# Sketched attention and a Swish-beta MLP on one core: the kernel rewritten with products on halves of the TensorE array, a key sum from ones columns, a first piece of 256 tokens, chunks of 512 tokens and a written order

## The chip, the cores and the metric

The kernel runs on one core of one Trainium2 chip. TensorE (PE) multiplies matrices into PSUM, its weight loads are profiled apart (PEld); VectorE (DVE) and ScalarE (ACT) read PSUM and SBUF, GpSimd (POOL) works on SBUF, SyncE (SP) issues most of the DMAs. The metric is the device time of one execution in microseconds. The kernel before took 153.2 us as the median of 3 runs (152.99 to 153.49).

## The reference

q, k and v are (4 batches, 4 heads, 1088 tokens, 32) float32, S1 and S2 are (8, 32). A sketch phi turns each 32-vector into 64 features, the attention is linear in them, and its output goes token by token into an MLP of width 2048.

```python
def phi(x):
    a = einsum('rd,bhsd->bhsr', S1, x)
    b = einsum('rd,bhsd->bhsr', S2, x)
    return einsum('bhsi,bhsj->bhsij', a, b).reshape(..., 64)
q_p, k_p = phi(q), phi(k)
kv  = einsum('bhsf,bhsd->bhfd', k_p, v)
z   = sum(k_p, axis=2)
num = einsum('bhsf,bhfd->bhsd', q_p, kv)
den = einsum('bhsf,bhf->bhs', q_p, z)[..., None] + 1e-06
x   = (num / den).transpose(0, 2, 1, 3).reshape(4352, 128)
h   = x @ w_in                                # (4352, 2048)
out = (h / (1 + exp(-beta * h))) @ w_out      # (4352, 128) float32
```

## The kernel before

The attention is computed in float32, the MLP in float16. A float32 matmul shows as two records in the profile, one for each of its two passes over the columns, and so do its weight loads; a float16 matmul shows as one.

Per batch, `attention(b)` makes a list of steps. Keys are transposed on VectorE in 32x32 blocks (`kT`, line 191), projected with S1 and S2 (`kproj`: `tk` or `tka`, line 216, nine matmuls, 128 weight columns, 64 moving columns), copied to SBUF (`tkS`) and multiplied to features `kp` (line 254, on POOL except in batch 0). `zt` (line 280, nine matmuls) and `wps` (line 298) make the key sum z in the form of eight more projection columns for the queries. `kvp` (line 314) adds up kv: 18 matmuls, of which those of heads 0 and 1 write PSUM partitions 0 to 63 and those of heads 2 and 3 partitions 64 to 127, so each uses 64 of the 128 columns of the array. Then three chunks of 384, 352 and 352 tokens of each head follow: `abp` (line 355) projects the queries, line 364 transposes that, lines 370 to 378 compute the denominator and divide, line 391 makes the query features `qp`, line 402 transposes them, and `xps` (line 411) multiplies them with kv in two accumulating matmuls. The result is cast to float16 as `xT`. In batch 0 the same tiles are called `abw` and `xw`, and ScalarE makes the copies.

`moe(b, ci)` takes one such chunk of 384 or 352 tokens through the MLP in eight waves: two matmuls into a `wave` of two PSUM banks (line 463), one Silu over both banks (line 466), and, two waves later, the two matmuls of the second product into `acc` (line 443). `winp` is w_in times beta and `woutp` is w_out divided by beta, so that Silu is all that is left. After the eighth wave `osb` (line 448) transposes `acc` and four DMAs write it out.

The order: attention of batch 0 is written whole ahead of the MLP; afterwards the steps of batch b+1 are spread evenly over the 24 waves of batch b, and a scheduler places the instructions of the engines by priority and readiness. The pools have two buffers of `wave`, of `att` and of `acc` in PSUM.

Of the kernel before, what the change touches and what calls it, by code (L numbers as in the profile page):

```python
# [10 lines left out]
ACTF = mybir.ActivationFunctionType  # L11

P = 128
# [4 lines left out]
def kernel(  # L18
# [12 lines left out]

# [4 lines left out]
    F = R * R  # L38
# [4 lines left out]
    assert DM == H * D == P and D == T and S == U * T and R == 8  # L43

    C = U // 4
    UL = U - 4 * C
    NB = C + 1
    assert UL == 2
    u_chk = []
    o = 0  # L50
    for n in (12, 11, 11):
        u_chk.append((o, n))
        o += n
    assert o == U
    NMAX = 12 * T

    const = ctx.enter_context(tc.tile_pool(name="const", bufs=1))
    sb = ctx.enter_context(tc.tile_pool(name="sb", bufs=2))
    ps = ctx.enter_context(tc.tile_pool(name="ps", bufs=2, space=bass.MemoryType.PSUM))

    def ap3(t, offset, dims):
        return bass.AP(tensor=t.tensor, offset=t.offset + offset, ap=[list(t.ap[0])] + dims)


    q_in = [const.tile([P, U * D], F32, tag=f"q_in{b}", name=f"q_in{b}") for b in range(B)]
    k_in = [const.tile([P, U * D], F32, tag=f"k_in{b}", name=f"k_in{b}") for b in range(B)]
    v_in = [const.tile([P, H, NB, D], F32, tag=f"v_in{b}", name=f"v_in{b}") for b in range(B)]
# [3 lines left out]
    def load_v(b, eng):  # L71
        for uu in range(4):
            eng.dma_start(
                out=v_in[b][T * uu : T * uu + T, :, 0:C, :].rearrange("p h c d -> p h (c d)"),
                in_=bass.AP(
                    tensor=v.tensor,
                    offset=v.offset + b * H * S * D + uu * C * D,
                    ap=[[U * D, T], [S * D, H], [1, C * D]],
                ),
            )  # L80
        for uu in range(UL):
            eng.dma_start(
                out=v_in[b][T * uu : T * uu + T, :, C, :],
                in_=bass.AP(
                    tensor=v.tensor,
                    offset=v.offset + b * H * S * D + (4 * C + uu) * D,
                    ap=[[U * D, T], [S * D, H], [1, D]],
                ),
            )

    nc.sync.dma_start(out=k_in[0], in_=k_rows[0])


    s_in = const.tile([P, P], F32, tag="s_in")
    nc.vector.memset(s_in, 0.0)
    s2bd = const.tile([2 * H * R, P], F32, tag="s2bd")
    nc.vector.memset(s2bd, 0.0)
    for h in range(H):
        nc.scalar.dma_start(out=s_in[T * h : T * h + R, T * h : T * h + T], in_=S1)
        nc.scalar.dma_start(out=s_in[T * h + R : T * h + 2 * R, T * h : T * h + T], in_=S2)  # L100
    load_v(0, nc.sync)
    nc.sync.dma_start(out=q_in[0], in_=q_rows[0])
    for h in range(H):
        nc.scalar.dma_start(out=s2bd[2 * R * h + R : 2 * R * h + 2 * R, T * h : T * h + T], in_=S2)


    bmask = const.tile([P, P], F32, tag="bmask")
    nc.gpsimd.memset(bmask, 0.0)
    for h in range(H):
        nc.gpsimd.memset(bmask[T * h : T * h + T, T * h : T * h + T], 1.0)  # L110
    zmask = const.tile([2 * H * R, H, R], F32, tag="zmask")
    nc.gpsimd.memset(zmask, 1.0)
    nc.gpsimd.affine_select(
        out=zmask, in_=zmask, pattern=[[-2 * R, H], [0, R]], base=0, channel_multiplier=1,
        compare_op=ALU.is_ge, fill=0.0,
    )
    nc.gpsimd.affine_select(
        out=zmask, in_=zmask, pattern=[[2 * R, H], [0, R]], base=2 * R - 1, channel_multiplier=-1,
        compare_op=ALU.is_ge, fill=0.0,
    )  # L120


    wq = []
    for i in range(2):
        w = const.tile([P, H, T], F32, tag=f"wq{i}", name=f"wq{i}")
        nc.vector.transpose(out=w.rearrange("p h r -> p (h r)"), in_=s_in)  # L126
        wq.append(w)
    prod = []
    for i in range(2):
        m = const.tile([P, 12, R + 1], F32, tag=f"prod{i}", name=f"prod{i}")  # L130
        nc.vector.memset(m[:, :, R : R + 1], 1e-6)
        prod.append(m)


    winp = const.tile([P, DFF], F16, tag="winp")
    woutp = const.tile([P, NJ, P], F16, tag="woutp")
    beta_bc = const.tile([P, DFF], F32, tag="beta_bc")
    w_in_sb = const.tile([P, DFF], F32, tag="w_in_sb")
    w_out_sb = const.tile([P, NJ, P], F32, tag="w_out_sb")
    betat = const.tile([P, NJ], F32, tag="betat")  # L140
    rbetat = const.tile([P, NJ], F32, tag="rbetat")
    nc.sync.dma_start(out=w_in_sb, in_=moe_w_in)
    nc.sync.dma_start(
        out=beta_bc,
        in_=bass.AP(tensor=moe_beta.tensor, offset=moe_beta.offset, ap=[[0, P], [1, DFF]]),
    )
    with nc.allow_non_contiguous_dma(reason="strided beta gather (one time)"):
        nc.scalar.dma_start(out=betat, in_=moe_beta.rearrange("(j p) -> p j", p=P))
    nc.sync.dma_start(out=w_out_sb, in_=moe_w_out.rearrange("(j p) m -> p j m", p=P))
    for b in range(1, B):  # L150
        nc.sync.dma_start(out=k_in[b], in_=k_rows[b])
        load_v(b, nc.sync)
        nc.sync.dma_start(out=q_in[b], in_=q_rows[b])
    HF = DFF // 2
    for i in range(2):
        nc.gpsimd.tensor_tensor(
            out=winp[:, i * HF : i * HF + HF],
            in0=w_in_sb[:, i * HF : i * HF + HF],
            in1=beta_bc[:, i * HF : i * HF + HF],
            op=ALU.mult,  # L160
        )

    def scale_w_out():
        nc.vector.reciprocal(out=rbetat, in_=betat)
        for j in range(NJ):
            nc.scalar.activation(
                out=woutp[:, j, :], in_=w_out_sb[:, j, :], func=ACTF.Copy, scale=rbetat[:, j : j + 1]
            )

    xts = {}  # L170


    def attention(b):
        first = b == 0
        st = {}
        steps = []

        def step(f):
            steps.append(f)

        def evac(o, i):
            if first:
                nc.scalar.copy(out=o, in_=i)  # L183
            else:
                nc.vector.tensor_copy(out=o, in_=i)  # L185

        @step
        def _():
            st["kT"] = sb.tile([P, U, T], F32, tag="kT", name="kT")
            kT = st["kT"]  # L190
            nc.vector.transpose(
                out=ap3(kT, 0, [[1, C * P]]), in_=ap3(k_in[b], 0, [[D, C], [C * D, 4], [1, D]])
            )
            nc.vector.transpose(
                out=ap3(kT, C * P, [[1, UL * T]]), in_=ap3(k_in[b], 4 * C * D, [[1, UL * D]])
# [36 lines left out]
        for c0 in range(0, NB, 3):  # L232
            @step
            def _(c0=c0):
                for c in range(c0, min(NB, c0 + 3)):
                    kproj(c)
# [280 lines left out]
```

## Time and profile before

| | |
|---|---|
| median of 3 runs | 153.2 us (152.99 to 153.49) |
| span of the profiled execution, first to last instruction | 151.3 us |
| outside of it, against the median | 1.9 us |
| PE busy | 125.2 us, 83% of the span |
| ScalarE busy / VectorE busy / POOL busy | 76.8 / 72.7 / 27.5 us |
| mean granted TensorE clock | 0.94 of full |
| first Silu ends | 50.7 us |
| last matmul ends | 146.8 us |

The profile gives no time of the profiled execution apart from its span, so the 1.9 us are the median less the span. Matmul rows overlap, since they are pipelined: what a group of matmuls costs is read from the chain of work that ended last, where a group's entry runs from its start to the next group's start. "x16" on a line is a count of records, two for each float32 matmul. The page's slices are 3.8 us each.

### The profile page before, as it was taken

To read this page: it belongs to the slowest core of one execution; us is meant where nothing else is said; L and a number is where in the kernel's file an instruction comes from. 1 tells how busy PE (TensorE), PEld (TensorE's weight loads), DVE (VectorE), ACT (ScalarE), POOL (GpSimd) and SP (SyncE) were. 2 spreads that over 40 slices of the span, in tenths; PEclk is the share of its full clock that TensorE was granted. 3 is DMA by queue.
4 is the path that set the end of the run, shared out by engine and by line. 5 is a ranking of instruction groups with operands and counts; after the bars stand their busy time and mean duration, and the time that the engine had idled before them with its cause. 6 is when DMAs were issued, how large, how long until landed. Compare 5 with 4: busy or idle time off the path is not lost.

```text
span 151.3 us, 2035 instructions
## 1 busy us (share of the span) xinstructions
PE 125.2 (83%) x752; PEld 78.3 (52%) x752; DVE 72.7 (48%) x163; ACT 76.8 (51%) x120; POOL 27.5 (18%) x33
## 2 busy tenths in 40 slices
PE   0058880959977599999999999999999999999970
PEld 0057750438553355655586565555865555555530
DVE  0313739085099904195922165965322857831110
ACT  0031039100102969884915487746335848669960
POOL 3023890005941000000009200000380000000000
PEclk9999996595599779999999999999999999999998
DMA  4649999996000000220200302020002020203122
GB/s 147 109 146 410 364 317 319 285 334 178 0 2 0 0 0 17 42 48 0 47 1 4 52 0 45 3 40 12 0 13 43 0 50 0 48 0 52 19 36 48
DMA packets 25866, 12.22 MB, mean 81 GB/s; under 512 B 22016, under 2 KB 24064, under 8 KB 25600
## 3 DMA queue, kind: packets, MB, share of 16 engines
q1 hardware_dynamic: 23600, 12.06, 29.4%
q10 hardware_dynamic: 2256, 0.02, 0.9%
q8 instruction: 6, 0.10, 0.3%
q14 instruction: 4, 0.03, 0.1%
HBM read 9.85 MB, written 2.23 MB: 80 GB/s over the span
## 4 chain that ended last, share of the span: by engine, by line
PE 60%; DVE 20%; ACT 9%; DMA 4%; issue 2%; ACTq 0%; DVEq 0%
PE wave L463 14%; PE acc L443 12%; PE xps L411 8%; ACT gT L466 8%; PE kvp L314 6%; PE xw L411 5%; DVE qp L391 4%; PE tka L216 4%; DMA betat<-in_moe_beta_dram 3%; DVE qpt L402 3%; PE abp L355 3%; PE zt L280 3%; DVE ab L364 3%; PE tk L216 2%; DVE kp L254 2%
## 5 line engine op out<-in xcount | busy, mean ns | idle before, releaser
L466 ACT ACTIVATE gT<-wave 128x704 f16<-128x704 f32 (+1 forms) x96 | 67.2, 775 | 29.2 <-PE wave L463 29.2
L463 PE MATMUL wave<-xT,winp 128*128 128x352 f16 (+1 forms) x192 | 46.9, 322 | 1.9 <-ACT gT L466 1.6
L443 PE MATMUL acc<-gT,woutp 128*128 128x352 f16 (+1 forms) x192 | 46.1, 322 | 0.2 <-ACT gT L466 0.2
L254 POOL TENSOR_TENSOR kp<-tkS 128x1024 f32<-128x1024 f32 (+2 forms) x11 | 15.7, 1453 | 75.0 <-DVE tkS L185 71.3
L463 PEld LDWEIGHTS <-winp 128*128 128x128 f16 x192 | 18.4, 99 | 19.6 <-issue 8.3
L443 PEld LDWEIGHTS <-woutp 128*128 128x128 f16 x192 | 18.7, 98 | 12.0 <-issue 1.8
L448 DVE STREAM_TRANSPOSE osb<-acc 128x352 f32<-128x352 f32 (+1 forms) x12 | 6.7, 558 | 16.6 <-PE acc L443 16.6
L411 PE MATMUL xps<-qpt,kv 128*128 128x352 f32 (+1 forms) x36 | 13.4, 489 | 0.4 <-DVE qpt L402 0.3
L185 DVE CAST xT<-xps 128x352 f16<-128x352 f32 (+1 forms) x9 | 4.8, 535 | 15.2 <-PE xps L411 15.2
L183 ACT CAST xT<-xw 128x352 f16<-128x352 f32 (+1 forms) x3 | 1.4, 461 | 21.0 <-PE xw L411 21.0
L391 DVE TENSOR_TENSOR qp<-an,ab 128x352 f32<-128x352 f32 (+1 forms) x24 | 11.8, 533 | 0.4
L314 PE MATMUL kvp<-kp,vc 128*64 128x128 f32 (+1 forms) x144 | 11.8, 311 | 0.0
L216 PE MATMUL tk<-wq,kT 128*128 128x64 f32 x16 | 3.7, 424 | 9.1 <-DVE wq L126 9.1
L402 DVE STREAM_TRANSPOSE qpt<-qp 128x704 f32<-128x704 f32 (+1 forms) x12 | 11.1, 922 | 0.3
L411 PE MATMUL xw<-qpt,kv 128*128 128x352 f32 (+1 forms) x12 | 7.0, 731 | 4.8 <-DVE qpt L402 4.8
L314 PEld LDWEIGHTS kvp<-kp,vc 128*64 128x64 f32 (+1 forms) x144 | 9.1, 156 | 2.6 <-issue 2.5
L411 PEld LDWEIGHTS xps<-qpt,kv 128*128 128x128 f32 x36 | 6.1, 189 | 5.1 <-DVE qpt L402 3.2
L216 PEld LDWEIGHTS tk<-wq,kT 128*128 128x128 f32 x16 | 3.5, 330 | 9.1 <-DVE wq L126 9.1
L280 PE MATMUL zt<-tkS 128*64 128x32 f32 (+1 forms) x72 | 7.2, 258 | 1.1 <-ACT tkS L183 0.7
L355 PE MATMUL abp<-qT,wq 128*128 128x352 f32 (+1 forms) x18 | 7.0, 472 | 1.1 <-DVE qT L307 1.1
L280 PEld LDWEIGHTS zt<-tkS 128*64 128x64 f32 (+1 forms) x72 | 6.4, 178 | 2.9 <-DVE tkS L185 1.1
L216 PEld LDWEIGHTS tka<-wq,kT 128*128 128x128 f32 x48 | 6.1, 202 | 3.3 <-issue 2.8
(49 smaller groups left out, 85.3 us busy)
## 6 DMA issues: line engine op xcount, KB each, us to landing
k_in<-in_k_dram SPq DMA_DIRECT2D x4, 544.0 KB, 3.8
q_in<-in_q_dram SPq DMA_DIRECT2D x4, 544.0 KB
v_in<-in_v_dram SPq DMA_DIRECT2D x16, 128.0 KB, 4.5
out_dram<-osb SPq DMA_DIRECT2D x32, 44.0 KB, 1.7
w_in_sb<-in_moe_w_in_dram SPq DMA_DIRECT2D x1, 1024.0 KB, 5.7
beta_bc<-in_moe_beta_dram SPq DMA_DIRECT2D x1, 1024.0 KB
out_dram<-osb SPq DMA_DIRECT2D x16, 48.0 KB, 1.8
s_in<-in_S_dram ACTq DMA_DIRECT2D x8, 1.0 KB
```

The source lines that it names most:

```text
L216: nc.tensor.matmul(out=st["tkp"][0][:, c * 64 : c * 64 + 64], lhsT=ap3(kT, c * P, [[1, P]]), rhs=wq[0][:, :, 0 : 2 * R], start=True, stop= ...
L254: eng.tensor_tensor(out=ap3(o, 0, [[F, nb * H], [R, R], [1, R]]), in0=ap3(t, 0, [[2 * R, nb * H], [1, R], [0, R]]), in1=ap3(t, R, [[2 * R, ...
L280: nc.tensor.matmul(out=zt[0 : 2 * H * R, 0 : H * R], lhsT=t, rhs=ap3(t, 0, [[2 * R, H], [1, R]]), start=(c == 0), stop=(c == NB - 1),)
L314: nc.tensor.matmul(out=st["kvp"][64 * p : 64 * p + 64, 0 : 2 * F], lhsT=st["vc"][:n, c, 2 * p : 2 * p + 2, :], rhs=st["kp"][:n, c, 2 * F * ...
L355: nc.tensor.matmul(out=abp[:, :n], lhsT=wq[b % 2].rearrange("p h r -> p (h r)"), rhs=st["qT"][:, u0 : u0 + un, :].rearrange("p u t -> p (u ...
L391: nc.vector.tensor_tensor(out=ap3(qp, fb * un * T, [[T, un], [R, 4], [1, R]]), in0=ap3(an, fb * 4, [[R, un], [1, 4], [0, R]]), in1=ap3(ab, ...
L402: nc.vector.transpose(out=ap3(qpt, 0, [[1, 2 * n]]), in_=ap3(st["qp", ci], 0, [[1, 2 * n]]))
L411: nc.tensor.matmul(out=xps[:, :n], lhsT=st["kv"][fb], rhs=ap3(qpt, fb * n, [[1, n]]), start=(fb == 0), stop=(fb == 1),)
L443: nc.tensor.matmul(out=acc[:, :n], lhsT=woutp[:, j, :], rhs=gT[:, j, :n], start=(j == 0), stop=(j == NJ - 1))
L448: nc.vector.transpose(out=osb[:, :un, :].rearrange("p u m -> p (u m)"), in_=acc[:, :n])
L463: nc.tensor.matmul(out=wave[:, jj, :n], lhsT=winp[:, j * P : j * P + P], rhs=x[:, :n], start=True, stop=True)
L466: nc.scalar.activation(out=gT[:, 2 * w : 2 * w + 2, :n], in_=wave[:, :, :n], func=ACTF.Silu)
```

## The change

The kernel is written anew; reference, inputs and types are the same.

- **Halves of the array.** The key projection takes 64 tokens as weights for each half of the columns, kv takes one head per matmul (64 weight columns, 64 moving columns), the query projection uses 64 of the 128 rows for each pair of heads, and the product with kv has 64 weight columns for each pair. Two matmuls that follow each other then lie on two halves. There is one product with kv per pair of heads in place of two accumulating ones.
- **z from ones columns.** Behind v in `v_in` lie 32 columns of ones, and the moving operand of the kv matmuls is v beside them, so z comes out of the same matmul. `zt` is gone; `W` (two small matmuls) stands for `wps`.
- **The first 256 tokens of batch 0** have features made by two projections (`fA`, `fB`) and a product, and are divided after the product with kv (`fden`, `frd`, `fR`, `fx`). The other 832 tokens of batch 0 go in two chunks of 416.
- **MLP chunks** are 256 tokens once and then eight times 512, over batch borders: 72 waves where there were 96. There is one `acc`, and two `wave` tiles of fixed banks.
- **Loads.** beta is loaded once (8 KB twice) and spread over partitions by matmuls with a row of ones (`bs`), and k, q and w_in of the start come in parts. Nine float16 matmuls on zeros (`filler`) stand at the start.
- **Written order.** Each engine's instructions are chained in the order of the code, by a table of slots (one slot is one wave): `plan`. ScalarE copies `tkS` and `xT` in all batches; POOL makes `kp` and `qp`.

```diff
+    def o(ins):
+        ...
+    wave = [pst(f"wave{i}", [P, 2, 512]) for i in range(2)]
+    att = pst("att", [P, 2, 512])
+    att1 = pst("att1", [P, 512])
+    acc = pst("acc", [P, 512])
...
-                nc.tensor.matmul(
-                    out=st["tkp"][0][:, c * 64 : c * 64 + 64],
-                    lhsT=ap3(kT, c * P, [[1, P]]),
-                    rhs=wq[0][:, :, 0 : 2 * R],
+                for th in range(2):
+                    mm(tkp[64 * th : 64 * th + 64, bank, 64 * cc : 64 * cc + 64],
+                       fap(kT[par], c * P + 64 * th, [[1, 64]]),
+                       wk.rearrange("p h s r -> p (h s r)"))
...
+        def kvmm(c, n):
+            ones_off = H * G * D
+            for hp in range(2):
+                for h2 in range(2):
+                    h = 2 * hp + h2
+                    off = (h * G + c) * D
+                    mm(att[64 * h2 : 64 * h2 + 64, hp, 0:64], kp[par][:, c, h, :],
+                       fap(v_in[b], off, [[ones_off - off, 2], [1, D]]),
+                       start=(n == 0), stop=(n == G - 1))
...
+            @step(f"qproj{key}")
+                for hp in range(2):
+                    pr = slice(64 * hp, 64 * hp + 64)
+                    mm(att[:, hp, 0:n], wqd[par][pr].rearrange("p a b r -> p (a b r)"),
+                       fap(qT[par][pr], u0 * T, [[1, n]]))
...
+            @step(f"num{key}")
+                for hp in range(2):
+                    mm(att1[64 * hp : 64 * hp + 64, 0:n], kvbd[par][:, hp, :, :].rearrange("p h d -> p (h d)"),
+                       fap(qpT[s], hp * n, [[1, n]]))
...
+    chunks = [(0, UF)] + [(u, 16) for u in range(UF, B * U, 16)]
...
+    filler(9)
+    run("st", "wk", "s2bd", "wqd", "kTa0")
+    for c in range(CA):
+        run(f"kproj0.{c}")
+    run("kTb0", "tka0")
...
+    run("fzc", "kvbd0", "zx0", "fden", "fnum", "frd", "fnS", "W0", "fR", "wev0", "fx", "qTb0")
+    for i in range(8):
+        run(f"wi{i}")
+    run("wo0A", "wo1A")
+    for i in (4, 5, 6, 7):
+        run(f"wo{i}P")
+    run("qproj0.0", "ab0.0", "den0.0", "an0.0V", "qproj0.1", "ab0.1", "qp0.0V", "den0.1", "an0.1V", "qp0.1V")
...
+    at(0, "wo2A", "qpT0.0")
+    at(2, "wo3A", "num0.0", "x0.0A", "qpT0.1")
+    at(5, "num0.1", "x0.1A")
+    def batch_plan(b, s, q):
+        at(s - 1, f"kT{b}")
+        at(s, *[f"kproj{b}.{c}" for c in range(0, 5)])
+        at(s + 1, *[f"kproj{b}.{c}" for c in range(5, G)], f"tk{b}")
+        at(s + 2, *[f"kp{b}.{c}-{c+2}P" for c in (0, 2, 4, 6)], f"kp{b}.8-9P", f"qT{b}")
+        for i, (c0, c1) in enumerate(((0, 2), (2, 4), (4, 6), (6, 8), (8, 9))):
+            at(s + 4 + i, ("kv", b, c0, c1))
+        at(s + 8, f"zx{b}", f"kvbd{b}", f"W{b}", f"wev{b}")
+        for i, (a, n) in enumerate(q):
+            at(a, f"qproj{b}.{i}", f"ab{b}.{i}")
+            ...
+            at(n, f"num{b}.{i}", f"x{b}.{i}A")
+    batch_plan(1, 2, [(10, 15), (13, 17), (15, 20)])
+    batch_plan(2, 18, [(26, 31), (29, 33), (31, 36)])
+    batch_plan(3, 34, [(42, 47), (48, 54), (55, 61)])
+    LAG = 2
+    for n in range(len(order) + LAG):
+        if n < len(order):
+            first_mm(*order[n])
+            silu(*order[n])
+        if n >= LAG:
+            second_mm(*order[n - LAG])
+        for p in plan.get(n, []):
+            ...
```

What moved on TensorE ahead of the first wave of the MLP. In the kernel before, this is the end of the start: `zt`, `wps`, `kvp` and `abp` here are batch 1's, `xw` is batch 0's second and third chunk.

```order
L411 MATMUL xw<-qpt,kv_234 128x352
L411 MATMUL xw<-qpt,kv_236 128x352
L355 MATMUL abw<-qT,wq_110 128x352
L280 MATMUL zt<-tkS 64x32
L298 MATMUL wps<-ztm,s2bd 128x32
L314 MATMUL kvp<-kp,vc 64x128 x18
L355 MATMUL abp<-qT,wq_112 128x384
L411 MATMUL xw<-qpt,kv_234 128x352
L411 MATMUL xw<-qpt,kv_236 128x352
L463 LDWEIGHTS winp
L463 MATMUL wave<-xT,winp 128x384
```

In the new kernel the same place holds only batch 0: kv with the spreading of beta (`bs`, the matmuls of `b_row`) between, the late division, and the query projection of the other 832 tokens (`att<-qT_77,wqd_87`); names without a number are the only or the first tile of that name, `att_123` is `att1`.

```order
L76 MATMUL att<-v_in_67,kp_81 64x64 x12
L76 MATMUL wave_121<-b_row,ones 128x512 x2
L76 MATMUL att<-v_in_67,kp_81 64x64 x24
L76 MATMUL wave_120<-zc,qpF 64x2 x8
L76 MATMUL wave_120<-qpF,kvbd_83 64x256 x2
L76 MATMUL att_123<-zx_85,s2bd 64x8 x2
L76 MATMUL wave_121<-ident,rdx 128x128 x2
L76 MATMUL att<-qT_77,wqd_87 128x416 x4
L76 LDWEIGHTS winp
L76 MATMUL wave_120<-xT,winp 128x256
```

Batch 1's projection and kv moved behind the first wave, and the product with kv of batch 0 (`xw` before, `num` now) has only the 256 tokens of `fnum` left ahead of it.

What moved on VectorE between the query projection and the product with kv, first chunk of batch 0. Before, one chunk of 384 tokens passes from `ab` to `qpt` by itself:

```order
L364 STREAM_TRANSPOSE ab<-abw 128x384
L370 TENSOR_TENSOR prod_114<-ab 128x12x8
L374 TENSOR_REDUCE den<-prod_114 128x12
L376 RECIPROCAL rden<-den 128x12
L378 TENSOR_TENSOR an<-ab,rden 128x96
L391 TENSOR_TENSOR qp<-an,ab 128x384 x2
L402 STREAM_TRANSPOSE qpt<-qp 128x768
```

Now two chunks of 416 tokens are interleaved, each with twice the columns, since the two pairs of heads lie side by side; `qpT_107` is what the first `num` reads.

```order
L79 TENSOR_TENSOR prod_92<-ab_89 128x26x8
L452 TENSOR_REDUCE den_95<-prod_92 128x26
L453 RECIPROCAL rden_98<-den_95 128x26
L79 TENSOR_TENSOR an_101<-ab_89,rden_98 128x104
L445 STREAM_TRANSPOSE ab_90<-att 128x832
L79 TENSOR_TENSOR qp_104<-an_101,ab_89 128x832
L79 TENSOR_TENSOR prod_93<-ab_90 128x26x8
L452 TENSOR_REDUCE den_96<-prod_93 128x26
L453 RECIPROCAL rden_99<-den_96 128x26
L79 TENSOR_TENSOR an_102<-ab_90,rden_99 128x104
L79 TENSOR_TENSOR qp_105<-an_102,ab_90 128x832
L472 STREAM_TRANSPOSE qpT_107<-qp_104 128x832
```

The second chunk's `ab`, denominator and `qp` moved ahead of the first chunk's last transpose.

What moved on TensorE among the waves of the MLP, where kv of a batch ends. Before, the last six kv matmuls of batch 2 stand between two waves, and the query projection comes three waves later:

```order
L443 LDWEIGHTS woutp
L443 MATMUL acc<-gT,woutp 128x352
L314 MATMUL kvp<-kp,vc 64x128 x6
L463 LDWEIGHTS winp
L463 MATMUL wave<-xT,winp 128x352
```

Now the last four kv matmuls of batch 2, `W` (`att_123<-zx_85,s2bd`) and the first query projection stand in one slot:

```order
L76 LDWEIGHTS woutp
L76 MATMUL acc<-gT_112,woutp 128x512
L76 MATMUL att<-v_in_69,kp_81 64x64 x4
L76 MATMUL att_123<-zx_85,s2bd 64x8 x2
L76 MATMUL att<-qT_77,wqd_87 128x320 x2
L76 LDWEIGHTS winp
L76 MATMUL wave_121<-xT,winp 128x512
```

`W` waits there for a VectorE product of kv's result, and the query projection for a VectorE product of `W`'s result, ahead of the next wave's matmuls.

826 lines of the change are left out of this document (445 added, 381 removed).

## The prediction

> **What bounds the kernel now.** I read the page's busy line and slices, then the chain of work that ended last, then groups by form. From the page:
>
> ```profile
> span 151.3 us, 2035 instructions
> PE   0058880959977599999999999999999999999970
> ACT  0031039100102969884915487746335848669960
> PEclk9999996595599779999999999999999999999998
> PE 60%; DVE 20%; ACT 9%; DMA 4%; issue 2%; ACTq 0%; DVEq 0%
> ```
>
> TensorE is full from about slice 14 to the end (3.8 us each), but ScalarE works steadily only from slice 13, that is from 48 us: about a third of the span passes before the MLP starts. The pieces of the chain (start, us, what) and two stretches (busy time of each engine in it, then granted clock):
>
> ```profile
> 9.13 3.68 PE tk L216 x16
> 17.35 3.83 PE kvp L314 x36
> 26.82 2.90 PE xw L411 x4
> 48.56 1.28 ACT L466
> 77.12 1.73 PE tka L216 x16
> 79.11 0.27 PE wave L463
> 80.01 1.28 PE zt L280 x18
> 81.86 0.33 PE wps L298 x2
> 82.78 0.81 PE kvp L314 x12
> 83.58 0.41 PE wave L463 x2
> 85.80 0.95 PE kvp L314 x12
> 87.45 0.30 PE wave L463 x2
> 88.05 0.65 PE abp L355 x2
> 88.70 0.30 PE wave L463 x2
> 92.97 1.51 PE xps L411 x4
> 98.75 1.47 PE xps L411 x4
> 105.95 1.73 PE tka L216 x16
> 135.68 5.23 ACT gT L466 x8
> 146.81 0.55 DVE osb L448
> ...
> 22.00:27.00 5.00, 0.18 (x1) 0.21 (x2) 4.47 (x10) 4.20 (x15) 0.61 (x1) 0.69 1.09 316
> 56.00:75.00 19.00, 18.96 (x106) 10.88 (x105) 11.07 (x24) 16.01 (x24) 0.00 (x0) 1.00 0.16 27
> ```
>
> Three stages. The start, up to 48.6 us: in 22 to 27 us TensorE works 0.18 us while VectorE makes the first chunk. The same 16 records of the key projection take 3.68 us at 9 us and 1.73 us at 77 us, so the array runs at half rate at first. The clock's digits read 9 there all the same; I go by durations. Then, to 135 us, TensorE bounds: batch to batch (77.12 to 105.95) is 28.8 us. Last, ScalarE paces at 5.23/8 = 0.65 us a wave.
>
> **The change, part by part.** I sum TensorE's work, since it runs in the written order and everything waits behind its waits.
>
> *MLP.* Two matmuls of 352 columns take 0.30 us, so a column costs 0.426 ns, and 32 x 4352 columns cost 59.3 us, whatever the chunk. A 512 wave costs 4 x 0.218 = 0.87 us. Wider chunks gain nothing here.
>
> *Attention of batches 1 to 3.* Before, by the chain: tk 2.0 (77.12 to 79.11), zt 1.28, wps 0.33, kv 2.6 (groups of 0.81 to 0.95), queries 1.85 (three of 0.65 or a little less), `xps` 4.4 (three of 1.47 to 1.51): 12.5 us a batch. Do halves run side by side? A 128-column pass takes about 0.65 / 768 x 128 = 0.108 us; the 12 records of `kvp` would take 1.30 us one after another and took 0.81 with both column halves in use. So yes for column halves. After, per batch:
> - key projection: 18 records on each half instead of 16 of full width. `zt` is the nearest row (64 weight columns, few moving): 18 in 1.28 us. In two slots, with one more entry: 1.5 us.
> - kv with z: 36 records on each half, 2 x 1.28 us, in five slots. A group's entry and leaving cost: `kvp` 0.81 against 6 x 0.108, and the wave behind it 0.41 against 0.30, so about 0.2 us; three more: 3.2 us.
> - `W`: as `wps`, 0.33 us.
> - queries: 64 rows per pair, two matmuls of the old length on row halves. No row shows row halves. Side by side they cost the old 1.85 us, one after another 3.7; I take the first, the row of column halves being nearest, plus three entries: 2.4 us, and keep 4.3 as the upper end. The Trainium skill has it in "TensorE: Matmul & The Clock Gate", Part 3: matmuls on different row groups run concurrently, four of them 3.07 times as fast as one by one; by that my sum stands, and no row here shows it.
> - product with kv: column halves, half of 4.4 less the waits, plus entries: 2.3 us.
>
> That is 9.7 us a batch, 29.1 in all, a gain of some 8 us.
>
> *The start.* Rows for it:
>
> ```profile
> 0.81 0.39 SPq L91 DMA_DIRECT2D k_in<-in_k_dram  x1
> 6.10 1.19 DVE L191 STREAM_TRANSPOSE kT<-k_in 128x1024 f32<-128x1024 f32 x1
> 13.89 2.27 PE L280 MATMUL zt<-tkS 128*64 128x32 f32 x18 [0.68 <-ACT tkS L183]
> ...
> L254 DVE TENSOR_TENSOR kp<-tkS 128x768 f32<-128x768 f32 x2 | 2.7, 1390 | 4.6 <-ACT tkS L183 4.6
> L183 ACT COPY tkS<-tk 128x512 f32<-128x512 f32 x1 | 0.6, 585 | 3.6 <-PE tk L224 3.6
> L364 DVE STREAM_TRANSPOSE ab<-abp 128x384 f32<-128x384 f32 x3 | 1.7, 583 | 2.3 <-PE abp L355 2.2
> L391 DVE TENSOR_TENSOR qp<-an,ab 128x384 f32<-128x384 f32 x8 | 4.1, 555 | 0.1
> L402 DVE STREAM_TRANSPOSE qpt<-qp 128x768 f32<-128x768 f32 x4 | 3.8, 956 | 0.1
> L374 DVE TENSOR_REDUCE den<-prod 128x12 f32<-128x108 f32 x4 | 1.0, 254 | 0.1
> ...
> k_in<-in_k_dram SPq DMA_DIRECT2D x4, 544.0 KB, 3.8
> out_dram<-osb SPq DMA_DIRECT2D x32, 44.0 KB, 1.7
> ```
>
> k lands 3.8 us after its issue at 0.81; the sketch matrices now come in two DMAs and not in twelve, so the first transpose starts at 4.7 and ends at 5.5 (640 columns at 1.19/1024). Projection at half rate by the cold `zt` row, 2.27 us for 18 records a half; the first copy is ready at 7.2. VectorE: 768 features 1.4, `wA`/`wB` 0.5, `qTa` 0.4: 9.5. `fA` and `fB`, four passes of 256 columns at half rate on each half: 11.2. `bs` twice 512 columns (1.7 in pairs), copies by ScalarE (1.2), kv of three blocks (0.6), `bs` again (1.7), kv of six (2.6): 19.0. Then the late division, each step behind the last: `zc`, `kvbd` and `zx` 0.8, `fden` 0.5, `frd` 0.7, `fR` 0.6, `fx` 0.4, `qTb` of 832 columns 1.0 (short VectorE steps by the reduce row's 0.25): 4.0, so 23.0. The first `qproj` 1.2 and its `ab` (832 columns, a little under the 0.583 of 384 scaled up: 1.05): 25.2. The first wave can only follow the second `qproj`, at about 26, against 48.6 before. But in slot 2 stands `num` of the first 416 tokens, which waits for the interleaved VectorE chain shown in the order: denominators 1.26 twice (four steps of 0.25 and a little for the double width), `ab` 1.05, `qp` 1.02 twice, `qpT` 1.0, which is 6.6 behind 25.2. So TensorE does two and a half short waves and then stands still until **32 us**.
>
> *From there*, TensorE's work: MLP 59.3 less the 8 short matmuls done, 58.4; the two `num` of batch 0, 1.7; attention 29.1: **89.2 us**.
>
> *Waits that the written order adds.* kv's end, `zx`, `W`, `wev` in one slot: two VectorE round trips, 0.75 a batch, 2.2. `kT` of batches 2 and 3 is queued on VectorE behind an `osb` and a `qpT` (0.7 + 1.0 + 1.3 before the projection that needs it, of which TensorE's other work covers 1.8): 1.2 twice, 2.4. One `acc` and not two: `osb` of 512 columns (0.7) lies ahead of the next chunk's second product, behind only 0.43 us of first product: eight times 0.1 to 0.3 us, 1.0. ScalarE's pace in some 30 waves without attention, 0.654 x 1024/704 = 0.95 against 0.87: 2.4. **8.0 us.** Before, the like was 28.8 less 12.5 and 14.8 us, 1.5 a batch. ScalarE in all: 68 full-wave equivalents of 0.95, 17 copies of 256 to 416 columns at 0.4 to 0.5 (by the 0.585 of 512): 72 us, beneath TensorE's 89. Its copies and Silu share one table load in the order, so none is added. POOL's work (kp 4.4 and qp 4.2 a batch by the row below) is hidden by the waves between.
>
> *Half rate after the stop at 32*: the chain shows TensorE's slow stretches ending only after some microseconds of unbroken work; at 5 us of it, **2.5 us** lost.
>
> *The end*: last Silu and product 0.7, `osb` 0.7 for 0.55, DMAs as before (146.81 + 0.55 to 151.3 is 3.9): **5.3 us**.
>
> Sum: 32 + 89.2 + 8.0 + 2.5 + 5.3 = 137.0 us of span, and with the 1.9 us by which the median lies above the profiled span, 138.9; I say **138.5 us**.
>
> **The rivals.**
> 1. *Row halves one after another.* Queries cost 1.85 more a batch (5.6), and in the start `qproj`, `fA`, `fB` and the pairs of `bs` cost 1.4 + 1.7 + 3.4, a part of it beside VectorE: about 10 us more, **148 us**. For it: no row shows rows split. Against: column halves pair off.
> 2. *The fillers keep the array at full rate.* Nine matmuls of 512 columns at half rate are 3.9 us unbroken work from about 1 us on. Then the start loses 1.1 at the projection, 0.9 at `fA`, 1.7 at `bs`, 1.6 at kv, 1.2 later, and the 2.5 after the stop: 9 us less, **129.5 us**. Against: from 9.13 to 21.2 us TensorE of the kernel before worked nearly without break, and kv at its end still took 3.83 us for 36 records where 12 take 0.81. The Trainium skill, "TensorE: Matmul & The Clock Gate", Part 1, says that one busy window of about 3.4 us releases the clock and an idle one throttles it; by that rule the fillers do release it, but the waits of the start give it back; the rows at 9 to 21 us agree only if gaps of half a microsecond spoil a window.
> 3. *POOL is late and TensorE waits at each `num`: slower than before.* The rows:
>
> ```profile
> L254 POOL TENSOR_TENSOR kp<-tkS 128x1024 f32<-128x1024 f32 x6 | 11.6, 1947 | 71.3 <-DVE tkS L185 71.3
> L254 POOL TENSOR_TENSOR kp<-tkS 128x512 f32<-128x512 f32 x1 | 1.8, 1831 | 3.7 <-ACT tkS L183 3.7
> ```
>
> A POOL product costs 1.9 ns an element alone, and 3.6 in the one row that ran beside VectorE's `kp`. From `qproj` to `num` lie four or five waves, some 5.3 us, and the way is `ab` 1.0, denominator 1.2, POOL 1.5, the next `ab` 1.0, `qpT` 1.0: 5.7, no slack. At 3.6 ns each of nine `qp` is 1.3 us later (11.7) and `kp` 3.8 a batch (11.4): 23 us if all is exposed, **161 us**. It decides from 15 of these 23 us on. Against: VectorE is busy only 11 of 19 us in a steady stretch, and not with products alone.
>
> **How the numbers follow.** My forecast as it stands, 131 to 145 us: 0.55. Rival 1: 0.17. Rival 2: 0.18. Rival 3 in full: 0.06; the rest, 0.04, is smaller mishaps of its kind. From 128 to 149 us lie the forecast, rival 2 and rival 1. Less than 0.3% either way is about what a measurement of this kernel cannot tell from no change; faster by more 0.93, the same 0.01, slower 0.06.
>
> **What would show it.** In the profile after: first Silu near 27 us and a wait of `num` for `qpT` of about 4 us right behind it; pairs of `qproj` of 384 columns in about 0.65 us (1.3 if rival 1); the 18 records of the projection in the first microseconds at 2.2 us or 1.1; kv groups of 16 records at about 0.7 us; TensorE over 90% busy from 33 us on, ScalarE about 70%; waits of `W` and of the projection for VectorE. I am wrong if waits for POOL come up in microseconds, if the start ends after 36 us, or if the steady stretch is bound by ScalarE.

## The result and the profile after

| | before | after |
|---|---|---|
| median of the runs, us | 153.16 (152.99 to 153.49) | 160.41 (159.0 to 161.63) |
| span of the profiled execution, us | 151.3 | 157.3 |
| first Silu of ScalarE starts, us from the span's start | 49.9 | 32.9 |
| from there to the end of the span, us | 101.5 | 124.4 |

The new kernel is slower: ratio 1.0411, 95% interval 1.033 to 1.0492. The forecast was 138.5 us. The profiled execution took 159.0 us, so 1.7 us lie outside its span. One of the four runs of the changed kernel (161.63 us) lies over 1.5% above its fastest; without it the median is 160.0, and differences to the changed kernel given below are some 0.4 us smaller. The four runs of one kernel here lie up to 3.2 us apart, so a difference of one or two microseconds between two versions is not clear.

The first Silu starts 17.0 us earlier (forecast: near 27 us, which would be 22.9); the rest of the program became 22.9 us longer. The kernel before loads a table on ScalarE right ahead of that Silu:

```profile
48.56 1.28 ACT L466 ACT_TABLE_LOAD   x1
49.86 2.21 ACT L466 ACTIVATE gT<-wave 128x768 f16<-128x768 f32 x3
```

The 48.6 us of the prediction is the start of this load. In the new kernel a load as long as this one starts at 2.1 us, far ahead of the first Silu, so 1.3 of the 17.0 us are this load and not the attention.

The page of the changed kernel, the slices (3.93 us each) of TensorE and of the granted clock:

```profile
PE   6539893673999898379998985599988869799950
PEclk9965568555599999955999999869999999999998
```

TensorE was to be over 90% busy from 33 us on. It falls to 3 and 7 tenths in slices 16 and 17 (counted from 0) and to 5 in slices 24 and 25. The clock's row reads 5 in slices 17 and 18 and 8 and 6 in slices 25 and 26, right behind these holes, and 5 or 6 through most of the start. The chain of work that ended last (start, us, what) shows the start and both holes:

```profile
7.22 0.83 PE wave L76 x20
8.55 0.71 PE wave L76 x16
11.12 2.08 PE wave L76 x8
16.38 1.55 PE att L76 x24
19.93 2.81 PE att L76 x48
27.65 1.78 PE att L76 x4
29.45 1.06 DVE ab L445
37.83 1.66 PE att L76 x4
...
55.81 0.87 PE att L76 x4
67.88 1.34 PE att L76 x20
69.21 0.97 PE wave L76 x2
73.91 0.84 PE att L76 x4
77.20 0.54 PE wave L76 x2
99.97 0.80 PE att L76 x20
104.89 0.80 PE att L76 x4
```

Up to 19.93 the rows are the key projection, `fA`/`fB` and kv of batch 0; then come the query projection (27.65 in batch 0, 55.81 in batch 1) and the product with kv, `num` (37.83, 73.91, 104.89); groups of 20 are the first part of a key projection. Behind the stop that ends at 67.88 a wave takes 0.97 us, where at full rate one takes 0.54 behind an attention group (77.20).

The waits by what ended them (engine, line, waited for: us in total, times, longest), of TensorE and one of VectorE:

```profile
PE att L76 <- DVE kT L337: 6.0, 2, 3.0
DVE qpT L472 <- POOL qp L79: 5.7, 7, 1.5
PE att L76 <- DVE qpT L472: 4.2, 3, 3.3
PE acc L76 <- DVE osb L580: 4.2, 5, 2.0
PE att L76 <- DVE wqd L79: 1.1, 3, 0.4
PE att L76 <- DVE zx L79: 1.0, 3, 0.3
```

The longest wait for `qpT`, 3.3 us, is that of the first `num`. After it the stops sum to 6.0 + 4.2 + 1.1 + 1.0 + 0.9 (the rest of `qpT`) and 0.9 for ScalarE's `xT` and `gT`: 14.1 us.

How VectorE comes to be late, in the timeline (start, us, engine, line, instruction, and in brackets the idle time before it):

```profile
63.50 0.71 DVE L580 STREAM_TRANSPOSE osb<-acc 128x512 f32<-128x512 f32 x1
63.66 1.51 POOL L79 TENSOR_TENSOR qp<-an,ab 128x768 f32<-128x768 f32 x1 [2.37 <-DVE an L79]
65.21 0.98 DVE L472 STREAM_TRANSPOSE qpT<-qp 128x768 f32<-128x768 f32 x1 [1.00 <-POOL qp L79]
66.11 2.06 DVE L337 STREAM_TRANSPOSE kT<-k_in 128x896 f32<-128x896 f32 x2
67.88 1.34 PE L76 MATMUL att<-wk,kT 128*64 128x64 f32 x20 [3.02 <-DVE kT L337]
```

`kT` takes 2.06 us and needs nothing but k, whose load ended long before; but it stands last on VectorE, behind `osb`, a wait of one microsecond for POOL, and `qpT`. The projection in turn stands ahead of the next wave on TensorE.

The stretch behind it (start to end, length, then busy time and instruction count of TensorE, its weight loads, VectorE, ScalarE and POOL, then granted clock, DMA share, GB/s):

```profile
67.80:72.00 4.20, 4.12 (x40) 2.52 (x40) 1.49 (x3) 1.02 (x1) 0.00 (x0) 0.50 0.00 0
```

TensorE is busy throughout, at a granted clock of 0.50. The clock's record has three such stretches after the first `num` began: 37.8 to 43.3, 67.2 to 74.0 and 101.3 to 104.7 us, with 15.0 us of TensorE's work in them. If half of that is lost to the rate, it is 7.5 us; by the waves (0.97 us and not 0.54) it is a little less. The first of them is the end of a stretch that began at 26.2 us, ahead of the stop before the first `num`; the other two follow the two stops for `kT`.

### The profile page after: what moved, and what is told of

Same layout as the page of the kernel before. It is cut to its first block, busy times and chain, and to the rows that moved or that the text cites. A ratio compares the mean times of both kernels' runs of the same rounds, so it can differ in the third digit from the quotient of the medians.

```text
span 157.3 us, 2314 instructions
## 1 busy us (share of the span) xinstructions
PE 123.5 (78%) x875; PEld 56.7 (36%) x875; DVE 62.4 (40%) x121; ACT 81.5 (52%) x107; POOL 41.8 (27%) x77
## 4 chain that ended last, share of the span: by engine, by line
PE 60%; DVE 23%; POOL 4%; ACT 3%; issue 3%; DMA 2%; ACTq 1%; DVEq 0%; POOLq 0%
PE att L76 25%; PE wave L76 21%; PE acc L76 15%; POOL qp L79 4%; DVE ab L445 4%; DVE qpT L472 3%; DVE kT L337 3%; DMA s_in<-in_S_dram 2%; ACT gT L568 2%; DVE osb L580 2%; DVE den L452 2%; DVE rden L453 1%; DVE prod L79 1%; DVE qp L79 1%; DVE an L79 1%
## 5 line engine op out<-in xcount | busy, mean ns | idle before, releaser
L568 ACT ACTIVATE gT<-wave 128x1024 f16<-128x1024 f32 (+1 forms) x72 | 66.9, 979 | 40.8 <-PE wave L76 40.2
L76 PE MATMUL acc<-gT,woutp 128*128 128x512 f16 (+1 forms) x144 | 43.2, 384 | 4.6 <-DVE osb L580 4.2
L76 PE MATMUL wave<-xT,winp 128*128 128x512 f16 (+1 forms) x144 | 43.6, 388 | 0.8 <-ACT xT L491 0.5
L79 POOL TENSOR_TENSOR qp<-an,ab 128x768 f32<-128x768 f32 (+1 forms) x9 | 12.9, 1437 | 53.5 <-DVE an L79 53.5
L79 POOL TENSOR_TENSOR kp<-tkS 128x512 f32<-128x512 f32 (+1 forms) x17 | 16.3, 988 | 34.5 <-ACT tkS L382 34.5
L445 DVE STREAM_TRANSPOSE ab<-att 128x768 f32<-128x768 f32 (+2 forms) x11 | 10.6, 959 | 16.8 <-PE att L76 16.8
L76 PE MATMUL att<-v_in,kp 128*64 128x64 f32 x288 | 14.0, 251 | 0.9 <-ACT beta_bc L303 0.9
L76 PEld LDWEIGHTS att<-v_in,kp 128*64 128x64 f32 x288 | 11.5, 159 | 8.1 <-issue 6.8
L76 PE MATMUL att<-qT,wqd 64*128 64x384 f32 (+2 forms) x44 | 11.4, 601 | 3.8 <-DVE qT L363 1.5
L472 DVE STREAM_TRANSPOSE qpT<-qp 128x768 f32<-128x768 f32 (+2 forms) x11 | 10.4, 942 | 5.7 <-POOL qp L79 5.7
```

The costliest lines, as they stand in the source:

```text
L76: o(nc.tensor.matmul(out=dst, lhsT=lhsT, rhs=rhs, start=start, stop=stop))
L79: o(eng.tensor_tensor(out=dst, in0=a, in1=b, op=op))
L445: o(V.transpose(out=fap(ab[s], 0, [[1, 2 * n]]), in_=att[:, :, 0:n]))
L472: o(V.transpose(out=fap(qpT[s], 0, [[1, 2 * n]]), in_=fap(qp[s], 0, [[1, 2 * n]])))
L568: o(A.activation(out=gT[ci % 2][:, 2 * w : 2 * w + 2, 0:n], in_=wave[w % 2][:, :, 0:n], func=ACTF.Silu))
```

## The experiments

The theory tested first (A in the expectations): nearly all of the loss against the forecast lies in stops of TensorE which the written order makes by what stands ahead in VectorE's queue, above all `kT`, and in the half rate that each long stop leaves behind it. The rival that had the right sign in the prediction is the third, POOL being late; others are that the new layout of `kT` itself is dear, and that the fillers matter. Each time is a median, with its ratio to the kernel before on the same chip and the 95% interval. Unless another is named, the edit is made to the changed kernel.

**e1: `kT` early.** VectorE transposes k of batches 2 and 3 eleven slots sooner.

```diff
-        at(s - 1, f"kT{b}")
+        at({1: 1, 2: 6, 3: 22}[b], f"kT{b}")
```

> The key transposes of batches 2 and 3 are written eleven slots earlier, where VectorE idles; nothing else changes. Theory A (TensorE stands 3.0 us twice for kT, and each stop drops the array to half rate for 6.8 and 3.4 us, which costs about half of that again): 160.4 less 6.0 less 4.7 = about 150 us, and no half rate after 45 us. Theory B (the query chain over VectorE and POOL is late by itself, kT only stands last in its queue): the projection starts earlier but num or acc wait instead, and 156 to 160 us remain.

Measured: 150.63 us, ratio 0.9862 (0.9765 to 0.9958): 9.8 us faster than the changed kernel, and now a little faster than the kernel before. The clock's row of the page:

```profile
PEclk9955555555558999999999999999999999999999
```

and the chain:

```profile
66.79 0.73 PE att L76 x20
70.08 0.80 PE att L76 x4
93.11 0.73 PE att L76 x20
```

The two holes for `kT` are gone, and with them the half rate behind them. From the projection of batch 2 to the `num` that follows it: 70.08 - 66.79 = 3.29 us here, 73.91 - 67.88 = 6.03 in the changed kernel (and 104.89 - 99.97 = 4.92 at batch 3). From batch 2's projection to batch 3's: 26.3 us here, 32.1 there. One entry of the plan was worth 6%: two stops, 6.0 us, and some 2.7 and 1.6 us of rate behind them (10.3 in all by the profiles, 9.8 by the medians). What VectorE waits for POOL has not changed; e1's wait:

```profile
DVE qpT L472 <- POOL qp L79: 5.7, 7, 1.5
```

**e2: the stops kept, and filled.** Matmuls of zeros into a PSUM bank that the next group clears anyway: 8 ahead of the first `num`, 14 ahead of the projection of batches 2 and 3. They leave nothing out of the computation.

```diff
+    def warm(bank, n):
+        for _ in range(n):
+            mm(bank, zero16[:, 0:P], zero16[:, 0:512])
...
-    at(2, "wo3A", "num0.0", "x0.0A", "qpT0.1")
+    at(2, "wo3A", "warm_num", "num0.0", "x0.0A", "qpT0.1")
...
         at(s - 1, f"kT{b}")
+        if b > 1:
+            at(s, f"warm_k{b}")
```

> All waits stay; zero matmuls on free PSUM banks fill the three long stops of TensorE (8 ahead of the first num, 14 ahead of the projection of batch 2 and of batch 3). Theory A (half rate behind a stop is a cost of its own): the granted clock stays full behind the stops of batches 2 and 3 and comes back earlier behind the first; 160.4 less up to 7.4 = 153 to 156 us. If the half rate costs nothing of its own, 160 us, or a little more for fillers that are longer than the stop.

Measured: 155.14 us, ratio 1.0194 (1.0064 to 1.0325), 5.3 us faster than the changed kernel by matmuls that compute nothing. The clock's row of the page:

```profile
PEclk9965555557999999999999999999999999999999
```

and the chain:

```profile
67.60 0.80 PE att L76 x20
70.95 0.80 PE att L76 x4
```

The projection still starts at 67.6 us, so the wait is there, but from it to `num` it takes 3.35 us and not 6.03. So the half rate behind a stop is a cost of its own (by e1's distances 1.6 and 2.7 us behind stops of 3.0), and e1's gain was not the stops alone.

**e5: `qp` on VectorE and not on POOL.** The rival of a late POOL.

```diff
-            at(a, f"den{b}.{i}", f"an{b}.{i}V", f"qp{b}.{i}P")
+            at(a, f"den{b}.{i}", f"an{b}.{i}V", f"qp{b}.{i}V")
```

> The query features of batches 1 to 3 are made on VectorE and not on POOL. Rival 3 of the prediction (POOL is late): the 5.7 us in which VectorE waits for POOL go, each product takes 0.9 us in place of 1.5, and the stops for kT and num shrink: 155 to 158 us. If VectorE is the one that is short, its queue gets 8 us longer and the time stays or rises: 160 to 164.

Measured: 160.89 us, ratio 1.0522 (1.0419 to 1.0625): no gain. TensorE's waits:

```profile
PE acc L76 <- DVE osb L580: 7.9, 5, 2.7
PE att L76 <- DVE kT L337: 3.8, 2, 1.9
```

VectorE no longer waits for POOL, and the stops for `kT` shrink from 6.0 to 3.8 us; but `osb` is now late and its stops grow from 4.2 to 7.9. What TensorE waits for is VectorE's queue; POOL's latency is only one of the things that stand in it. The edit trades a wait for work of VectorE's own (0.93 us for a product), so it shows that taking `qp` off POOL is no cure, and not what the waits for POOL cost by themselves. That POOL is not the main cause follows from e1, which is 9.8 us faster with the same 5.7 us of waits for POOL.

**e3 and e11: `kT` in contiguous rows.** In the changed kernel the transposes write every fourth element; here they write runs, and v is loaded in the partition order that belongs to it.

```diff
-    kT = [sbt(f"kT{i}", [P, G, T, 4]) for i in range(2)]
+    kT = [sbt(f"kT{i}", [P, G, 4, T]) for i in range(2)]
...
-            dma(eng, fap(vt, h * G * D, [[1, G * D]]), dram(v, src, [[U * D, T], [G * D, 4], [1, G * D]]))
+            dma(eng, fap(vt, h * G * D, [[1, G * D]]), dram(v, src, [[G * D, 4], [U * D, T], [1, G * D]]))
...
-                        out=fap(kT[par], x0 * P, [[1, nj], [P, x1 - x0], [4, T]]),
+                        out=fap(kT[par], x0 * P, [[P, x1 - x0], [T, nj], [1, T]]),
```

> kT is written in contiguous runs of 32 tokens in place of a step of four elements, with v loaded in the matching order of partitions. If the step doubles the transposes (2.1 us for a batch now, 1.35 for the same columns in the kernel before), a batch takes about 1.4 us, the two stops for kT shrink by 0.7 each, the start by 0.5: about 158.5 us. If the time is the number of blocks and not the step, 160.4.

Measured: 159.94 us, ratio 1.044 (1.0304 to 1.0575): not to be told from the changed kernel. A group by form (line, engine, instruction, count, busy us, mean ns) of the changed kernel:

```profile
L337 DVE STREAM_TRANSPOSE kT<-k_in 128x896 f32<-128x896 f32 x3 | 5.2, 1727 | 0.0
```

the same group of e3:

```profile
L337 DVE STREAM_TRANSPOSE kT<-k_in 128x896 f32<-128x896 f32 x3 | 3.2, 1069 | 0.0
```

and one of e3's waits, and the clock's row of its page:

```profile
PE att L76 <- DMA b_row<-in_moe_beta_dram: 1.9, 1, 1.9
PEclk9955555555569999987999999689999969999995
```

The 896 columns that the first part of a projection waits for cost 1.07 us and not 1.73, so the layout with a step of four in the output is what the prediction's 1.3 us for a whole batch missed (the edit changes the order in which the input is read along with it). The two stops shrink (4.7 us and not 6.0), but TensorE now waits 1.9 us in the start for `b_row`, which the changed kernel does not. That the reordered loads of v delay it is likely and was not tried by itself. And in the profiled run a third stretch of half rate appears (the 6 in slice 32; 128.2 to 131.6 us), right behind a stop of 1.98 us for `osb` (125.25 to 127.23). The changed kernel has the same stop at 125.19 to 127.16 us and goes on at full rate. The same edit on top of e8 below:

> As e8_all, with kT written in contiguous runs as in e3_kt_rows. There the transposes shrank from 2.1 to 1.4 us a batch without a gain in time. If VectorE's length is what is left: 0.5 less at the start, 143.5 us; if the matching order of v's loads costs what the transposes gain: 144 to 145.

Measured: 144.72 us, ratio 0.9468 (0.9377 to 0.956), against 144.14 without it: where the stops for `kT` are gone already, nothing is won that these runs could show.

**e4: no fillers.** The nine matmuls of zeros at the very start are left out; they compute nothing.

```diff
-    filler(9)
```

> The changed kernel without the nine matmuls on zeros at its start. In the profile after, the clock is full from 5.7 to 9.1 us and half from there to 22.8: the fillers bring the projection of batch 0 (1.5 us for both parts) to full rate and are lost again. Without them it takes 3 us: 160.4 plus about 1.5 = 162 us. If the fillers carry the start (rival 2 of the prediction), 165 or more; if they do nothing, 160.4.

Measured: 159.77 us, ratio 1.0424 (1.0321 to 1.0527), the same as with them. The chain:

```profile
7.17 1.36 PE wave L76 x20
9.03 1.15 PE wave L76 x16
20.84 2.81 PE att L76 x48
```

The fillers do what they are for: the first projection took 0.83 and 0.71 us with them and takes 1.36 and 1.15 without. But TensorE then waits for copies and VectorE, and kv's last 48 records take 2.81 us in both kernels, half rate by e9 below. Nine fillers warm the array for work worth one microsecond; the first `num` starts at 38.73 us without them and at 37.83 with them, which is within the spread of the runs.

**e6: `osb` out of the way.** e1 with the query projections of the second and third chunk of batch 3 two and three slots later (their `num` one and two), so that `osb` is not queued behind them.

```diff
-    batch_plan(3, 34, [(42, 47), (48, 54), (55, 61)])
+    batch_plan(3, 34, [(42, 47), (50, 55), (58, 63)])
```

> As e1_kt_early, and the second and third query chunk of batch 3 stand two and three slots later, so that VectorE has the output transposes of the chunks that end in slots 49 and 57 ahead of them and not behind them. Theory A (the single acc makes TensorE wait for a transpose that is queued behind the query chain: 1.98 and 0.88 us in the profile): e1 less 2.5 = 148 us. If those waits only move on to num: as e1, 150.6.

Measured: 150.22 us, ratio 0.9817 (0.9716 to 0.9917); e1 gave 0.9862. TensorE's waits:

```profile
PE att L76 <- DVE qpT L472: 5.4, 5, 3.3
PE acc L76 <- DVE osb L580: 2.1, 5, 0.5
PE wave L76 <- ACT xT L491: 1.7, 3, 0.6
```

The wait for `osb` halves (it is 4.2 us in e1 as in the changed kernel), that for `qpT` grows from 4.2 to 5.4, and that for `xT` from 0.5 to 1.7. The wait only moves on.

**e7: a shorter way to the first `num`.** e1 with `qTb0` ahead of the late division, and with the first chunk of batch 0 alone up to `qpT`, the second following behind the first wave.

```diff
-    run("fzc", "kvbd0", "zx0", "fden", "fnum", "frd", "fnS", "W0", "fR", "wev0", "fx", "qTb0")
+    run("qTb0", "fzc", "kvbd0", "zx0", "fden", "fnum", "frd", "fnS", "W0", "fR", "wev0", "fx")
...
-    run("qproj0.0", "ab0.0", "den0.0", "an0.0V", "qproj0.1", "ab0.1", "qp0.0V", "den0.1", "an0.1V", "qp0.1V")
+    run("qproj0.0", "ab0.0", "den0.0", "an0.0V", "qp0.0V", "qpT0.0")
...
-    at(0, "wo2A", "qpT0.0")
-    at(2, "wo3A", "num0.0", "x0.0A", "qpT0.1")
+    at(0, "wo2A", "qproj0.1", "ab0.1")
+    at(2, "wo3A", "num0.0", "x0.0A", "den0.1", "an0.1V", "qp0.1V", "qpT0.1")
```

> As e1_kt_early, and in the start the 832 query columns are transposed ahead of the late division, the first chunk of 416 tokens runs through VectorE to its last transpose before the second chunk begins, and the second chunk's projection stands behind the first wave. Theory A (the start ends when VectorE's interleaved chain does): first wave at about 28 us and not 32, first num at about 33 and not 38, its wait of 3.3 us gone: e1 less 5 = about 145.5 us. If TensorE at half rate is what sets the start, num comes only 1 to 2 us earlier: 149.

Measured: 145.86 us, ratio 0.9532 (0.9447 to 0.9618), 4.8 us better than e1. The first `num` in the timeline:

```profile
34.09 1.65 PE L76 MATMUL att<-qpT,kvbd 128*64 128x416 f32 x4 [0.55 <-DVE qpT L472]
```

It begins at 34.09 us and waits 0.55 us for `qpT`, against 39.34 and 3.28 in the profile of e1 (37.83 and 3.3 in the changed kernel). Here the written order was the cause again, not the amount of work; the two changes of order were not tried apart.

**e8: e6 and e7 together,** and `kT` of batch 1 transposed in the start, behind `qTb0`. Beside e7:

```diff
-    run("qTb0", "fzc", "kvbd0", "zx0", "fden", "fnum", "frd", "fnS", "W0", "fR", "wev0", "fx")
+    run("qTb0", "kT1", "fzc", "kvbd0", "zx0", "fden", "fnum", "frd", "fnS", "W0", "fR", "wev0", "fx")
...
-        at({1: 1, 2: 6, 3: 22}[b], f"kT{b}")
+        if b > 1:
+            at({2: 6, 3: 22}[b], f"kT{b}")
...
-    batch_plan(3, 34, [(42, 47), (48, 54), (55, 61)])
+    batch_plan(3, 34, [(42, 47), (50, 55), (58, 63)])
```

> e1, e6 and e7 together, and the key transpose of batch 1 written into the start, where VectorE waits for kv. If the three costs are independent: 150.6 less 2.5, less 5, less 1 = about 142 us, 7% under the kernel before; if one hides another: 145 to 147.

Measured: 144.14 us, ratio 0.9421 (0.9335 to 0.9506), 1.7 us better than e7; the two intervals overlap. Against e1, e6 gave 0.4 us and e7 4.8; the three edits together give 6.5, and not the 8.5 that were expected of them. The first `num` is no earlier here than in e7 (34.65 us). What the earlier `kT` of batch 1 is worth by itself was not tried.

**e9: e8, and the stops of the start filled.** Matmuls of zeros into `acc`, which its first product clears: 15 at the beginning and not 9, and 2, 7, 3 and 4 in four later stops.

```diff
-    filler(9)
+    filler(15)
...
+    filler(2)
...
+    filler(7)
...
+    filler(3)
...
+    filler(4)
```

> As e8_all, with matmuls on zeros in every stop of TensorE in the start (15 at first in place of 9, then 2, 7, 3 and 4). If the half rate lengthens the start by itself (projections, spreading of beta, kv and late division are some 12 us of matmuls at half rate): 4 to 6 us less, 138 to 140 us. If the start is set by VectorE, ScalarE and the loads: 143 to 145.

Measured: 139.65 us, ratio 0.9174 (0.9074 to 0.9274). This is the fastest version of the study, faster than the kernel before by 8% and than the changed kernel by 13%. Its timeline:

```profile
16.41 1.62 PE L76 MATMUL att<-v_in,kp 128*64 128x64 f32 x48
20.39 0.63 PE L76 MATMUL wave<-zc,qpF 128*64 128x2 f32 x16 [2.37 <-DVE zc L79]
24.49 0.60 ACT L568 ACTIVATE gT<-wave 128x512 f16<-128x512 f32 x1 [1.19 <-PE wave L76]
28.98 0.92 PE L76 MATMUL att<-qpT,kvbd 128*64 128x416 f32 x4 [1.97 <-DVE qpT L472]
29.91 1.29 PE L76 MATMUL att<-wk,kT 128*64 128x64 f32 x20
```

kv takes 1.62 us for its 48 records and not 2.81, and the first Silu starts at 24.5 us. Half rate in the start was worth 4.5 us. The 2.4 us that TensorE waits for `zc` come from `kT` of batch 1, which stands ahead of it on VectorE and waits 3.5 us for its load; putting it elsewhere was not tried. That 139.65 us lies near the forecast's 138.5 is chance: it is another order of the kernel, with filled stops.

**e10: the same in the kernel before.** 26 matmuls of zeros ahead of its first key projection, nothing else.

```diff
+    for _ in range(26):
+        nc.tensor.matmul(out=zacc, lhsT=zero16[:, 0:P], rhs=zero16, start=True, stop=True)
```

> The kernel before with 26 matmuls on zeros ahead of its first key projection, one part of the change alone. Its projection, key sum and kv of batch 0 take 10 us at half rate (3.68, 2.27 and 3.83 us against 1.73, 1.28 and 2.4 later). If the fillers bring full rate into that stretch: 153.2 less 4 to 5 = 148 to 149 us. If that stretch loses the full rate again, or the start waits for VectorE: 152 to 153.5.

Measured: 152.79 us, ratio 1.0011 (0.9956 to 1.0065): no change. Its chain:

```profile
9.74 1.85 PE tk L222 x16
15.98 4.26 PE kvp L320 x36
```

`tk` takes half of the 3.68 us it took, but `kvp` still takes longer (4.26) than the 3.83 of the kernel before, and the span stays. Warming the array once is worth nothing if the next stop undoes it, or if TensorE was not what the start waited for; this run doesn't tell the two apart.

## Why the prediction was wrong

The forecast's sum against the changed kernel's profile, in us of span:

| term of the prediction | forecast | measured |
|---|---|---|
| start until the first `num` | 32.0 | 37.8 |
| TensorE's work from there, with ScalarE's pace | 89.2 + 2.4 | 92.6 (the rest of the span) |
| waits that the written order adds, without ScalarE's pace | 5.6 | 14.1 |
| half rate | 2.5 | 7.5 |
| the end (measured: behind the last matmul) | 5.3 | 5.3 |
| span | 137.0 | 157.3 |

*What was right.* TensorE's work. Row halves run side by side: the query projection's four records of 384 columns take 0.87 us with the group's entry, where twice the old 0.65 would be 1.30, so rival 1 does not hold. That agrees with what the Trainium skill has in "TensorE: Matmul & The Clock Gate", Part 3, on row groups. A kv group of 16 records takes 0.62 us (about 0.7 forecast), `num` 0.80 to 0.87, the waits for `zx` and `W` 2.1 (2.2 forecast), and the end is as forecast in sum (`osb` and the DMAs alone take the 5.3 us, where the forecast had 4.6 for them and 0.7 for the last Silu and product, which stand in the rows above here). ScalarE is not the bound: from the first `num` on it is busy for 72.2 of 119.5 us, 60%.

*First step that failed: "Waits that the written order adds".* The `kT` term was 2.4 us and measured 6.0, and e1 shows that these 6.0 us go when `kT` alone is moved. Its mechanism was right (queued behind `osb` and `qpT`), its sizes were not. At batch 2, from the start of `osb` (63.50) to the projection (67.88) it is 4.4 us and not 3.0: the `qpT` ahead of `kT` itself waits 1.0 us for POOL, which the prediction left out of that queue though it knew `qp` to be there, and the part of `kT` that the projection needs takes 1.73 us and not 1.3, because of its layout (e3). And TensorE's other work covers 1.35 us of it (until 64.85) and not 1.8. The `acc` term was 1.0 and measured 4.2: priced as eight equal delays of 0.1 to 0.3 us, it is in fact single delays of up to 1.98 us, where `osb` comes behind a chunk of attention in VectorE's queue. No run wins these back: e6 halves them, and TensorE waits elsewhere.

*Second: "Half rate after the stop at 32", 2.5 us.* It counted one stretch, and had that about right (half of the 5.5 us of work from 37.8 to 43.3 is 2.7), but the stops for `kT` have the same effect: 7.5 us of loss in three stretches. A wait of 3.0 us so costs 4.6 to 5.7 us (e1's 3.29 us against 4.92 and 6.03). e1 takes away two stops and their rate (9.8 us), e2 only the rate behind three (5.3 us).

*Third: the start.* It was priced link by link, and most links were late by a little: the projection begins at 7.22 and not 5.5 (S lands at 5.2 us, later than k was forecast to, and `kTa` has the step of four as well: 1.23 us in the chain); `fA` begins at 11.1 (9.5); kv ends at 22.7 (19.0), since its first three blocks take 1.55 us and not 0.6; the query projection begins at 27.65 (23.0); the first chain of VectorE from its `ab` to `num` takes 7.3 (6.6). Of the start as it is, the half rate is worth 4.5 us (e9), and the two chunks woven into each other at its end together with the late `qTb0` 4.8 (e7). But the prediction had both in its 32 us, so they are not what made the start 5.8 us later than forecast; that stays a sum of small sizes which no run takes apart.

*The rivals.* Rival 3 had the sign but not the cause, and that its 161 us lie near the measured 160.4 is luck: POOL's waits exist (5.7 us on VectorE, 1.0 of them in the queue ahead of each of the two late `kT`), but with `qp` on VectorE nothing is gained (e5), and with the waits kept e1 gains 9.8 us. Rival 2 is refuted by e4 in the form in which the kernel has it; with more of the stops filled its idea holds (e9). The row halves of rival 1 do pair off. The range's upper end, 149, stood on rival 1 and had no room for several waits of the same queue being late together, each with its half rate. Two of the signs of being wrong came true: the start ended after 36 us, and waits for POOL came up in microseconds.

*Seen from the kernel before:* the stretch from the first Silu on grew from 101.5 to 124.4 us. Take off the wait before the first `num`, the later stops and the rate (3.3 + 14.1 + 7.5) and 99.5 is left. The kernel before, whose TensorE stands for only 1.6 us between its first Silu and its last matmul, had 101.5. So about as much is left as before, although batch 1's key projection, its kv and the products with kv for the later tokens of batch 0 were moved into this stretch: by this sum the cheaper products paid for that, which no run shows alone. The gain of the start was real and was given back by the order.

## What to carry to other kernels

Where engines run in a written order, price each wait by what stands ahead of it in the other engine's queue, including what that work waits for itself; work that needs only old data, such as `kT` here, goes where that queue is idle. Behind every stop of TensorE of about 3 us, add a stretch of 3.4 to 6.8 us at half rate, as it was here; where a stop can't be removed, matmuls of zeros into a free bank, up to the real work, give the rate back (e2, e9), while warming the array once at the beginning gained nothing (e4, e10).

## What was not expected of the hardware

- A stop of 3.0 us halved TensorE's rate for one or two stretches of some 3.4 us (101.3 to 104.7, 67.2 to 74.0), and the half rate can set in behind the first work after the stop (at 101.3, where the stop ended at 99.97). A stop of about 2 us may or may not do it: in the changed kernel and in e1 pairs of matmuls go on at 0.43 us behind a stop of 1.98 us for `osb`, while in e3 the same stop is followed by pairs at 0.85 us, and in e9 the projection behind a stop of 1.97 us takes 1.29 us for 20 records and not 0.80. The lengths agree with the windows of about 3.4 us in the Trainium skill, "TensorE: Matmul & The Clock Gate", Part 1. That part has the rate fall after one idle window of that length; here shorter stops were enough, and the measurement decides.
- The same part of the Trainium skill takes the ramp for less than 1% of a typical kernel's span. In the start of e8 alone, half rate cost 4.5 of 144.1 us, 3% (e9), and the measurement decides. From the first `num` of the changed kernel on, it was another 7.5 of 157.3 us, 5%.
- Matmuls of zeros count as work for the rate (e2 and e9).
- Transposing 128x896 on VectorE takes 1727 ns with an output step of four elements and 1069 ns with contiguous runs of output (e3, where the order of the input changes too).
- The clock's row is not always to be trusted: in e4 the digits read 9 at 7 us, as at full speed, while the projection that took 0.83 us in the changed kernel took 1.36. In e8 they read 9 all through the start, though its 48 records of kv take the 2.81 us of half rate. Durations decide.
